# First slot's row list from match matrices, strided q and k loaded as runs of two tokens, idle matmuls at the head, low words on VectorE

## The chip, the core and the metric

One core of a Trainium2 chip runs one program. TensorE (PE in the profile) multiplies, VectorE (DVE) and ScalarE (ACT) do the elementwise work and empty PSUM, GpSimd (POOL) does some elementwise work and issues the indirect DMAs (gather, scatter), and SyncE (SP) issues most plain DMAs. Each engine takes its instructions in the order in which they were planned. The metric is the device time of one execution in microseconds; lower is better.

## The reference, cut to what matters

```python
B, H, S, HD = 4, 8, 576, 64
# heads 0-3: local mask, 32 wide; heads 4-7: strided mask, same position modulo 32
attn = softmax(where(mask, q @ k.T / 8, -1e9)) @ v
x = attn.transpose(0, 2, 1, 3).reshape(2304, 512)
logits = x @ w_gate                       # 512 x 8
e = argmax(logits); gate = softmax(logits)[e]; g2 = sigmoid((x @ w_output_gate)[e])
y[t] = gate[t] * g2[t] * relu(x[t] @ w1[e]) @ w2[e]          # per token, one expert of 8
h = relu(y @ w_in); out = (h * h) @ w_out                     # 512 -> 2048 -> 512
```

## The kernel before

**Attention.** Four batches b. Each loads q, k, v (`load`, L232), turns q and k on TensorE and empties PSUM by `evac` (`transposes`, L276), and then runs units: nine "l" units for the local heads in five steps, and four pieces a0, a1, b0, b1 for the strided heads. `unit` and `piece_s`/`unit_s` make scores and softmax, `unit2` turns the probabilities, `unit3` multiplies by v and writes the result, transposed, to `xT`. The order of the steps is written in `ORDER`; `evac` gives every second copy to ScalarE and every second to VectorE. In the strided heads one partition holds 18 neighbouring tokens, so the transposed tiles `qsT`, `ksT`, `qlT`, `klT` are written with a stride of nine words.

**Routing, in the same stage.** Whenever 128 tokens are complete, `gates` (L499) multiplies them by the identity and the gate weights (`rw`, L509), empties them to `xr`, adds up the logits (`lg`), and stores the rows to `x_d` in DRAM (SP, L529). Tokens go in four groups, `GROUPS = [(0,4),(4,9),(9,13),(13,18)]`. `route` (L661) picks the expert, and counts each token's place in its expert's list (`posi`, through the matmuls `rk`). `scatter` (L730, POOL) writes token numbers at these places into the table `tab_d` in DRAM.

**The first slot.** After tile 12, `largest` (L572) finds the expert that has most tokens so far. Its list of rows is read back from `tab_d` (`rows_of`, L543), its first 208 rows are gathered from `x_d` (`win_get`, L547), and turned to `xh`, `xl` (L614 to L618). The rest of the slot comes from the last five tiles without a list: `late_rows` (L631) multiplies their high and low words `xa`, `xb` by match matrices `pm` (L649), on top of the gathered rows' own part (L623). `early_load` (L558) issues the list, the first two weight chunks `r` and the gathers, and is called by the scatter of tile 12. Its tiles lie where the front part of the attention's memory was.

**The experts.** Eight slots, in falling order of their counts; three-pass fp32r matmuls (`mm3`, L970 to L972) with high words `hw` from ScalarE (L950) and low words `lw` from VectorE (L954). Then the last two layers by a two-level scheme of seven products.

**What sets the order around the change.** A planner places every instruction by its own estimate of time; `tc.issue_after` pins one behind another on its engine. In the code before, the first two `hw` follow the last attention unit's copy, and the `lw` follow the last `pm`. The low words `xb` of tiles 13 to 17 are GpSimd's (`LPOOL`).

Of the kernel before, what the change touches and what calls it, by code (L numbers as in the profile page):

```python
# [20 lines left out]
P = 128  # L21
# [37 lines left out]
LPOOL = (13, 14, 15, 16, 17)  # L59
# [3 lines left out]
LWP = 0  # L63

# [28 lines left out]
C_END = C_TRI + P  # L93
# [3 lines left out]
def make_consts():  # L97
# [13 lines left out]
    c[:, C_TRI : C_TRI + P] = p[:, None] < p[None, :]  # L111
    c[:, C_IDX : C_IDX + NTILE] = p[:, None] + P * np.arange(NTILE)[None, :]
# [12 lines left out]
def moe_kernel(ctx, tc, q, k, v, wg, wog, w1, w2, w_in64, w_out64, consts, out, dbg=None):  # L125
# [9 lines left out]
    msk = big.tile([P, C_END - C_ML], F32, name="msk")  # L135
# [3 lines left out]
    ident = cst[:, C_ID : C_ID + P]  # L139
    cstb = big.tile([P, C_END - C_BF], BF16, name="cstb")  # L140
# [3 lines left out]
    trib = cstb[:, C_TRI - C_BF :]  # L144
    onesb = big.tile([P, P], BF16, name="onesb")
    nc.vector.memset(onesb, 1.0)
# [22 lines left out]
    zrow = big.tile([1, D], F32, name="zrow")  # L169
# [54 lines left out]
    for i in range(NPT):  # L224
# [5 lines left out]
        nc.vector.memset(x, 0.0)  # L230
# [4 lines left out]
    def load(b):  # L235
# [4 lines left out]
        for nm, src in (("q", q), ("k", k)):  # L240
            t[nm + "s"] = x = fro.tile([P, NS * HD], F32, name=f"{nm}s{b}", tag=nm + "s", bufs=1)
# [32 lines left out]
    def transposes(b, t):  # L274
        t.update(trs[b % 2])
        for kind in "sl":  # L276
            for n0 in range(0, 9, 3):
                for nm in ("q", "k"):
# [3 lines left out]
                    for i in range(3):  # L282
# [5 lines left out]
                        nc.tensor.transpose(ps[:, i, :], src, ident)  # L288
# [9 lines left out]
                    evac(y.rearrange("d h (g n) -> d n h g", n=9)[:, n0 : n0 + 3], z, 0.125 if nm == "q" else None)  # L298
# [53 lines left out]
    def piece_s(b, t, u, a):  # L352
# [3 lines left out]
        if a == 0:  # L356
            scs[b, u] = pss.tile(G, F32, name=f"sc{nm}", tag="sc")
            nc.tensor.matmul(
                flat(scs[b, u]),
                identb,  # L360
# [1078 lines left out]
```

## Time and profile before

| | us |
|---|---|
| median of 3 runs | 808.07 (807.59 to 809.14) |
| the profiled execution, its own time | 810.12 |
| its span in the profile | 808.2 |
| TensorE busy | 755.3 (93%) |
| VectorE busy | 554.9 (69%) |
| ScalarE busy | 467.4 (58%) |
| GpSimd busy | 192.1 (24%) |
| mean granted TensorE clock | 0.984 |

The span is the time between the first and the last instruction that the profiler shows; 1.9 us lie around it. TensorE's busy time contains pipelined matmuls whose ends are modelled, so a busy TensorE may still be waiting a little. The granted clock is 1.00 at 2.4 GHz and 0.50 at 1.2 GHz.

### The profile page before, as it was taken

To read this page: it belongs to the slowest core of one execution; us is meant where nothing else is said; L and a number is where in the kernel's file an instruction comes from. 1 tells how busy PE (TensorE), PEld (TensorE's weight loads), DVE (VectorE), ACT (ScalarE), POOL (GpSimd) and SP (SyncE) were. 2 spreads that over 40 slices of the span, in tenths; PEclk is the share of its full clock that TensorE was granted. 3 is DMA by queue.
4 is the path that set the end of the run, shared out by engine and by line. 5 is a ranking of instruction groups with operands and counts; after the bars stand their busy time and mean duration, and the time that the engine had idled before them with its cause. 6 is when DMAs were issued, how large, how long until landed. Compare 5 with 4: busy or idle time off the path is not lost.

```text
span 808.2 us, 14396 instructions
## 1 busy us (share of the span) xinstructions
PE 755.3 (93%) x5355; PEld 679.8 (84%) x5355; DVE 554.9 (69%) x1034; ACT 467.4 (58%) x930; POOL 192.1 (24%) x183
## 2 busy tenths in 40 slices
PE   4789999499999999999989999999999999999994
PEld 3667777499999999999977888888898988899893
DVE  6758867554548578779898778787554688566542
ACT  3746746234546456656686667666655586556443
POOL 4102122635075654531132221004000003000002
PEclk9999999689999999999999999999999999999998
DMA  9995611729479998976545633524232225212002
GB/s 193 202 194 146 142 54 29 237 71 340 165 174 292 172 331 295 309 248 198 178 170 161 210 125 127 177 87 150 92 106 89 72 98 182 86 73 97 21 1 82
DMA packets 105410, 124.83 MB, mean 154 GB/s; under 512 B 42801, under 2 KB 77137, under 8 KB 105330
## 3 DMA queue, kind: packets, MB, share of 16 engines
q1 hardware_dynamic: 95746, 100.77, 42.9%
q0 software_dynamic: 8096, 22.63, 8.5%
q8 instruction: 44, 0.72, 0.4%
q10 hardware_dynamic: 1488, 0.42, 0.2%
q14 instruction: 36, 0.29, 0.2%
HBM read 101.67 MB, written 22.12 MB: 153 GB/s over the span
## 4 chain that ended last, share of the span: by engine, by line
PE 53%; issue 17%; DMA 10%; DVE 9%; ACT 5%; POOL 4%; SPq 1%; POOLq 0%; ACTq 0%; DVEq 0%
PE o L970 4%; PE o L972 4%; DMA s0wo<-in_moe_w_out_dram 4%; PE o L971 4%; PE h L970 3%; PE h L971 3%; PE h L972 3%; PE y L970 3%; PE y L971 3%; PE y L972 3%; PE rw L509 2%; DMA ws_d<-sa 1%; POOL idx_d L862 1%; DMA idx_d<-toki,cpi 1%; PE lr L649 1%
## 5 line engine op out<-in xcount | busy, mean ns | idle before, releaser
L970 PE MATMUL o<-hwo,gh 128*128 128x512 f32 x288 | 114.5, 398 | 5.1 <-ACT gh L1098 5.1
L971 PE MATMUL o<-lwo,gh 128*128 128x512 f32 x288 | 113.4, 394 | 0.0
L954 DVE TENSOR_TENSOR lw<-rw,hw 128x1024 fp32r<-128x1024 f32 x62 | 79.0, 1274 | 44.6 <-ACT hw L950 41.6
L1184 ACT ACTIVATE rl<-rl 128x384 f32<-128x384 f32 x96 | 49.5, 518 | 94.7 <-DVE rl L1182 94.6
L950 ACT ACTIVATE hw<-rw 128x1024 fp32r<-128x1024 f32 x62 | 65.8, 1062 | 65.5 <-PE h L971 44.8
L972 PE MATMUL o<-hwo,gl 128*128 128x512 f32 x288 | 85.1, 396 | 2.0 <-DVE gl L1099 2.0
L1099 DVE TENSOR_TENSOR gl<-rl,gh 128x384 fp32r<-128x384 f32 x96 | 58.0, 606 | 41.9 <-ACT gh L1098 40.8
L1215 POOL DMA_INDIRECT out_dram<-ob,idx x18 | 20.6, 1147 | 273.9 <-ACT ob L1214 269.2
L970 PE MATMUL h<-xh,hw 128*128 128x416 f32 (+7 forms) x256 | 81.0, 316 | 1.5 <-DVE hl L1070 1.3
L972 PE MATMUL h<-xh,lw 128*128 128x416 f32 (+7 forms) x256 | 79.4, 310 | 0.0
L971 PE MATMUL h<-xl,hw 128*128 128x416 f32 (+7 forms) x256 | 79.4, 310 | 0.0
L971 PE MATMUL y<-hl,hw 128*128 128x416 f32 (+7 forms) x256 | 77.1, 310 | 0.0
L972 PE MATMUL y<-hh,lw 128*128 128x416 f32 (+7 forms) x256 | 76.6, 310 | 0.0
L970 PEld LDWEIGHTS o<-hwo,gh 128*128 128x128 f32 x288 | 54.0, 188 | 17.6 <-ACT gh L1098 8.6
L970 PE MATMUL y<-hh,hw 128*128 128x416 f32 (+7 forms) x256 | 68.0, 311 | 0.2 <-ACT hh L1069 0.2
L972 PEld LDWEIGHTS o<-hwo,gl 128*128 128x128 f32 x288 | 53.6, 188 | 13.1 <-DVE gl L1099 3.4
L971 PEld LDWEIGHTS o<-lwo,gh 128*128 128x128 f32 x288 | 54.1, 188 | 9.0
L1098 ACT ACTIVATE gh<-rl 128x384 fp32r<-128x384 f32 x96 | 49.9, 521 | 1.8
L970 PEld LDWEIGHTS h<-xh,hw 128*128 128x128 f32 x256 | 48.1, 188 | 3.2 <-DVE hl L1070 2.9
L1185 ACT ACTIVATE rl<-rl 128x384 f32<-128x384 f32 x96 | 49.5, 519 | 1.7
L971 PEld LDWEIGHTS h<-xl,hw 128*128 128x128 f32 x256 | 48.2, 188 | 0.3 <-DVE xl L659 0.2
L971 PEld LDWEIGHTS y<-hl,hw 128*128 128x128 f32 x256 | 48.1, 188 | 0.1
(597 smaller groups left out, 1917.4 us busy)
## 6 DMA issues: line engine op xcount, KB each, us to landing
rw<-in_moe_w_dram SPq DMA_DIRECT2D x62, 512.0 KB
rwa<-ws_d SPq DMA_DIRECT2D x24, 512.0 KB
rwb<-ws_d SPq DMA_DIRECT2D x24, 384.0 KB
e6wi<-in_moe_w_in_dram SPq DMA_DIRECT2D x32, 256.0 KB
rwo<-wout_d SPq DMA_DIRECT2D x16, 512.0 KB
x_d<-xr SPq DMA_DIRECT2D x18, 256.0 KB
ws_d<-eo POOLq DMA_DIRECT2D x16, 256.0 KB, 4.9
s0wo<-in_moe_w_out_dram SPq DMA_DIRECT2D x8, 512.0 KB
```

The source lines that it names most:

```text
L509: nc.tensor.matmul(ps[:, kk, :], xT[:, kd, col : col + P], igw[:, kd, :], start=True, stop=True)
L649: nc.tensor.matmul(ps[:, a, :], parts[t][x][:, 2 * h + a, :], pm, start=False, stop=(t == NTILE - 1 and a == x == 1),)
L950: nc.scalar.activation(hi, raw, AF.Copy)
L954: eng.tensor_tensor(lo, raw, hi.bitcast(F32), op=ALU.subtract)
L970: kept(nc.tensor.matmul(ps, ah, bh, start=first, stop=False))
L971: kept(nc.tensor.matmul(ps, ah, bl_, start=False, stop=False))
L972: kept(nc.tensor.matmul(ps, al, bh, start=False, stop=last))
L1098: nc.scalar.activation(h, x, AF.Copy)
L1099: nc.vector.tensor_tensor(l, x, h.bitcast(F32), op=ALU.subtract)
L1184: nc.scalar.activation(rl[:, :HC], src, AF.Relu)
L1185: nc.scalar.activation(rl[:, :HC], rl[:, :HC], AF.Square)
L1215: ins = nc.gpsimd.indirect_dma_start(out=out[:, :], out_offset=bass.IndirectOffsetOnAxis(ap=idx[:, gt_, 0:1], axis=0), in_=ob, in_offset=None,
```

## The change

- **Row list.** `match_tiles` makes, for each tile below 13, a 128 x 128 matrix that marks the low seven bits of each token's place (`pmh`), and keeps the rest (`posm`). `match_rows` compares the rest with the list's columns, multiplies by token numbers, and adds 13 small matmuls into one PSUM tile, from which `ix0` is made. The first slot no longer reads `tab_d`. `early_load` moves out of the scatter to the main loop, and the scatters of the last two groups follow the gathers on GpSimd (`put_place`).
- **Strided q and k.** A partition holds nine runs of two tokens (512 bytes); each tensor is loaded by four DMAs, one a head, where there was one of 4608 bytes a partition. The transposed tiles are then written without a stride; `ksT` has its two halves apart. The local heads' q and k are laid out alike. Batch 0's strided k goes through ScalarE's queue.
- **Idle matmuls.** `turn_over` issues 10 matmuls of 512 columns ahead of everything, and two after each group of batch 0's strided transposes.
- **Low words.** `xb` is VectorE's for all of tiles 13 to 17; those of 16 and 17 follow the last `pm`.
- **Order.** The first two `hw` follow the last `xa`; the first slot's transposes follow the last `rw`; some memsets move to GpSimd; slot 1's transposes come one step later.

```diff
-LPOOL = (13, 14, 15, 16, 17)
+LPM = (16, 17)
+HEAD = (10, 2)
...
+    pairs = lambda src, b, h: src[b, 4 + h].rearrange("(n g u) d -> g n (u d)", g=32, u=2)
+    ks0 = fro.tile([P, S * 4 // P * HD], F32, name="ks0", tag="ks", bufs=1)
+    for h in (0, 2, 1, 3):
+        nc.scalar.dma_start(ks0[32 * h : 32 * h + 32].rearrange("p (n c) -> p n c", c=2 * HD), pairs(k, 0, h))
...
+    def turn_over(n, ins=None):
+        for _ in range(n):
+            with tc.issue_after(ins.ins) if ins else nullcontext():
+                ins = nc.tensor.matmul(
+                    idle, onesb, onesb[:, None, :].to_broadcast([P, 4, P]), start=True, stop=True
+                )
+
+    turn_over(HEAD[0])
...
-            go(x, src[b, 4:8].rearrange("h (g n) d -> (h g) (n d)", n=NS))
+            for h in (0, 2, 1, 3):
+                go(x[32 * h : 32 * h + 32].rearrange("p (n c) -> p n c", c=2 * HD), pairs(src, b, h))
...
-                go(x[h // 2 * HD : h // 2 * HD + HD, :, h % 2, :], src[b, h].rearrange("(g n) d -> g n d", n=NL_))
+                go(x[h // 2 * HD : h // 2 * HD + HD, :, h % 2, :], src[b, h].rearrange("(n g) d -> g n d", n=NL_))
...
-                        y = y.rearrange("d h (g n) u -> d n h g u", n=9)[:, n0 : n0 + 3]
+                        y = y.rearrange("d h u (n g) -> d u n h g", n=9)[:, :, n0 : n0 + 3]
                         for j in range(2):
                             r = slice(j * HD, (j + 1) * HD)
-                            evac(y[r, :, :, :, j], z[r])
+                            evac(y[r, j], z[r])
...
-                nc.scalar.activation(xa, xr[:, :, :P], AF.Copy)
-                eng = nc.gpsimd if t in LPOOL else nc.vector
-                eng.tensor_tensor(xb, xr[:, :, :P], xa.bitcast(F32), op=ALU.subtract)
+                lead["xa"] = nc.scalar.activation(xa, xr[:, :, :P], AF.Copy)
+                low = lambda xa=xa, xb=xb, xr=xr: nc.vector.tensor_tensor(
+                    xb, xr[:, :, :P], xa.bitcast(F32), op=ALU.subtract
+                )
...
+    def match_tiles(b, ts):
+        T = len(ts)
+        sl = slice(ts[0], ts[0] + T)
+        hi = wk.tile([P, 5], I32, name=f"hi{b}", tag="hi", bufs=1)
+        nc.vector.tensor_scalar(hi[:, :T], posi[:, sl], P - 1, None, op0=ALU.bitwise_and)
+        hf = wk.tile([P, 5], F32, name=f"hf{b}", tag="hf", bufs=1)
+        nc.vector.tensor_copy(hf[:, :T], hi[:, :T])
+        for i, t in enumerate(ts):
+            nc.vector.tensor_scalar(
+                pmh[:, t, :], cstb[:, C_IA - C_BF : C_TK - C_BF], hf[:, i : i + 1], None, op0=ALU.is_equal
+            )
+        nc.vector.tensor_tensor(posm[:, sl], posi[:, sl], hf[:, :T], op=ALU.subtract)
...
+    def match_rows():
+        rel = wk.tile([P, LATE], F32, name="relm", tag="relm", bufs=1)
+        nc.vector.tensor_scalar(rel, posm, lead["base"], None, op0=ALU.subtract)
...
+        for t in range(LATE):
+            nc.tensor.matmul(
+                ips.rearrange("p e r -> p (e r)"),
+                pmh[:, t, :],
+                wt[:, t].rearrange("p e r -> p (e r)"),
+                start=(t == 0),
+                stop=(t == LATE - 1),
+            )
...
     def early_load():
+        match_rows()
         e0 = lead["e0"]
         oreg[0] = nc.values_load(e0[0:1, :], engines=[ET.SP], min_val=0, max_val=E - 1)
-        lead["ix"] = rows_of(0, oreg[0])
...
-                for a in range(KD):
-                    nc.tensor.transpose(ps[:, a, :c], w[:c, a, :], ident[:c, :c])
+                with tc.issue_after(lead["rw"].ins):
+                    for a in range(KD):
+                        nc.tensor.transpose(ps[:, a, :c], w[:c, a, :], ident[:c, :c])
...
+        with tc.issue_after(lead["pm"].ins):
+            while lows:
+                lows.pop(0)()
...
-            if t == LATE - 1:
-                early_load()
...
-        with tc.issue_after(last_ev["s"].ins) if first else nullcontext():
+        with tc.issue_after(lead["xa"].ins) if first else nullcontext():
             nc.scalar.activation(hi, raw, AF.Copy)
...
-            if f == 4 and k + 1 < E:
+            if f == (5 if k == 0 else 4) and k + 1 < E:
                 win_split(k + 1)
```

## Rows read from the trace of the kernel before

**Rows 1.** Busy time by stretch: span, then PE, PEld, DVE, ACT, POOL, clock, DMA share, GB/s
```profile
0.00:26.20 26.20, 12.74 (x173) 8.93 (x173) 17.68 (x33) 8.30 (x11) 10.01 (x15) 1.00 1.00 209
...
42.00:142.90 100.90, 94.56 (x1418) 74.16 (x1418) 75.37 (x239) 58.53 (x192) 17.73 (x21) 1.00 0.49 110
142.90:169.00 26.10, 15.53 (x80) 14.63 (x81) 12.85 (x23) 6.05 (x11) 15.57 (x14) 0.61 0.57 184
169.00:808.00 639.00, 619.49 (x3490) 571.82 (x3488) 437.90 (x712) 381.44 (x668) 146.67 (x130) 1.00 0.50 157
```

**Rows 2.** Chain that ended last, 140 to 170 us: start, length, what
```profile
140.70 2.17 PE rw L509 x16
...
157.50 3.85 PE lr L623 x16
161.47 7.72 PE lr L649 x40
```

**Rows 3.** Timeline, the first slot's list: start, length, engine, line, operation, idle before it
```profile
130.58 0.18 DVE L697 TENSOR_REDUCE posi<-pp 128x4 int32<-128x32 f32 x1
132.64 0.15 DVE L595 TENSOR_REDUCE base<-tb 128x1 f32<-128x8 f32 x1
...
135.12 0.97 POOL L730 DMA_INDIRECT tab_d<-tok,posi  x1 [0.30 <-issue]
...
141.14 0.44 SPq L543 DMA_DIRECT2D ix<-tab_d  x1
...
145.30 0.99 POOL L547 DMA_INDIRECT win<-x_d,ix  x1 [9.21 <-issue]
...
151.34 1.12 PE L614 MATMUL wt<-cst,win 128*128 128x128 f32 x4 [8.49 <-DMA win<-x_d,ix]
```

**Rows 4.** Busy time of a 2 us stretch inside the gap
```profile
148.00:150.00 2.00, 0.00 (x0) 0.00 (x0) 0.26 (x1) 1.56 (x4) 1.69 (x2) 0.50 1.12 333
```

**Rows 5.** Timeline, the last group's route and the first slot's words
```profile
146.71 1.06 ACT L950 ACTIVATE hw<-r 128x1024 fp32r<-128x1024 f32 x1 [5.49 <-DMA r<-in_moe_w_dram]
...
150.01 6.17 POOL L519 TENSOR_TENSOR xb<-xr,xa 128x512 fp32r<-128x512 f32 x5
...
150.70 0.20 DVE L665 TENSOR_REDUCE mx<-lg 128x5 f32<-128x40 f32 x1
150.93 5.31 DVE L667 TENSOR_TENSOR d<-lg,mx 128x40 f32<-128x40 f32 x1
...
158.27 1.31 DVE L637 TENSOR_SCALAR pm<-cst,rel 128x208 fp32r<-128x208 f32 x5
...
159.50 1.08 DVE L618 TENSOR_TENSOR xl<-wt,xh 128x512 fp32r<-128x512 f32 x2
...
160.50 2.35 DVE L954 TENSOR_TENSOR lw<-r,hw 128x1024 fp32r<-128x1024 f32 x2
```

**Rows 6.** Timeline, small bf16 matmuls on one PSUM tile
```profile
129.83 0.22 PE L684 MATMUL rk<-oh,onesb 128*128 128x24 bf16 x3
```

**Rows 7.** Groups by shape, ScalarE: copies with and without a stride, mean ns
```profile
L272 ACT ACTIVATE ksT<-ts1k 64x384 f32<-64x384 f32 x3 | 2.7, 890 | 0.1
...
L272 ACT ACTIVATE pts2l<-pt2l 96x512 f32<-96x512 f32 x3 | 1.8, 592 | 0.5 <-PE pt2l L409 0.5
```

**Rows 8.** Timeline and waits at the head: three transposes each, and TensorE's waits
```profile
5.26 0.90 PE L288 MATMUL ts0q<-cst,qs 128*128 128x128 f32 x3 [5.26 <-DMA cst<-in_consts_dram]
...
26.28 0.52 PE L288 MATMUL ts1q<-cst,qs 128*128 128x128 f32 x3 [3.27 <-DMA qs<-in_q_dram]
```

**Rows 9.** Waits of TensorE, 26 to 143 us: waited in total, times, longest
```profile
PE tl1q L288 <- DMA vsp<-in_v_dram: 1.6, 1, 1.6
```

**Rows 10.** DMA queue: packets, MB, share of 16 engines; in 0.5:5, 9:15 and 108:121 us
```profile
q1 hardware_dynamic: 211, 0.90, 53.9%
...
q1 hardware_dynamic: 3349, 1.04, 121.8%
...
q1 hardware_dynamic: 1023, 0.51, 13.1%
```

More of the change, by code (lines that the diff above doesn't have):

```diff
@@ L92 @@
 C_TRI = C_MS + SM
[L93 removed]
+C_IA = C_TRI + P
+C_TK = C_IA + P
+C_END = C_TK + 2 * LATE
 C_BF = C_ML - P
@@ L287, in transposes @@
                             src = x[:, n].rearrange("p j d -> p (j d)")
-                        nc.tensor.transpose(ps[:, i, :], src, ident)
+                        ins = nc.tensor.transpose(ps[:, i, :], src, ident)
+                    if b == 0 and kind == "s":
+                        turn_over(HEAD[1], ins)
+                        lead["ts"] = ins
                     y = t[nm + kind + "T"]
@@ L357, in piece_s @@
             scs[b, u] = pss.tile(G, F32, name=f"sc{nm}", tag="sc")
-            nc.tensor.matmul(
-                flat(scs[b, u]),
-                identb,
-                cstb[:, None, C_MS - C_BF : C_MS - C_BF + SM].to_broadcast([P, n_s, SM]),
-                start=True,
-                stop=False,
-            )
+            with tc.issue_after(lead["ts"].ins) if b == 0 else nullcontext():
+                nc.tensor.matmul(
+                    flat(scs[b, u]),
+                    identb,
+                    cstb[:, None, C_MS - C_BF : C_MS - C_BF + SM].to_broadcast([P, n_s, SM]),
+                    start=True,
+                    stop=False,
+                )
         sc = scs[b, u]
@@ L473, in drain, with put_place @@
                 while scq:
-                    scq.pop(0)[1]()
+                    put_place()
+    def put_place():
+        _, fn, g = scq.pop(0)
+        with tc.issue_after((last_ev["p"] if g < 2 else lead["win"]).ins):
+            fn()
     carry = [None]
@@ new lines, in match_rows @@
+    def match_rows():
+        rel = wk.tile([P, LATE], F32, name="relm", tag="relm", bufs=1)
+        nc.vector.tensor_scalar(rel, posm, lead["base"], None, op0=ALU.subtract)
+        eq = wk.tile([P, LATE, NW], F32, name="eqm", tag="eqm", bufs=1)
+        nc.vector.tensor_tensor(
+            eq,
+            rel[:, :, None].to_broadcast([P, LATE, NW]),
+            cst[:, None, C_PJ : C_PJ + NW].to_broadcast([P, LATE, NW]),
+            op=ALU.is_equal,
+        )
+        wt = wk.tile([P, LATE, 2, NW], BF16, name="wtm", tag="wtm", bufs=1)
+        tk = cstb[:, C_TK - C_BF : C_END - C_BF].rearrange("p (t e) -> p t e", e=2)
+        nc.vector.tensor_tensor(
+            wt,
+            eq[:, :, None, :].to_broadcast([P, LATE, 2, NW]),
+            tk[:, :, :, None].to_broadcast([P, LATE, 2, NW]),
+            op=ALU.mult,
+        )
+        ips = pss.tile([P, 2, NW], F32, name="ips", tag="tp")
+        for t in range(LATE):
+            nc.tensor.matmul(
+                ips.rearrange("p e r -> p (e r)"),
[3 more added lines that the diff above has]
+                stop=(t == LATE - 1),
+            )
+        lead["ix"] = ix = const.tile([P, NW], I32, name="ix0")
+        i2 = wk.tile([P, NW], F32, name="i2", tag="i2", bufs=1)
+        nc.vector.tensor_copy(i2, ips[:, 1])
+        nc.vector.scalar_tensor_tensor(out=ix, in0=ips[:, 0], scalar=float(P), in1=i2, op0=ALU.mult, op1=ALU.add)
@@ L697, in route @@
             nc.vector.tensor_reduce(posi[:, ts[0] : ts[0] + T], pp[:, :T], axis=AX.X, op=ALU.add)
+        if ts[0] < LATE:
+            match_tiles(b, ts)
         cn = wk.tile([P, E], F32, name=f"cn{b}", tag="cn", bufs=2)
@@ L779, in moe_kernel @@
                 )
-            if scq and nun[0] >= scq[0][0] and (b < B - 1 or "ok" in lead):
-                with tc.issue_after(last_ev["p"].ins):
-                    scq.pop(0)[1]()
+            if b == B - 1 and n >= LN and early and "do" in lead:
+                lead.pop("do")()
+                early_load()
+                lead["ok"] = 1
+            if scq and nun[0] >= scq[0][0] and (scq[0][2] < 2 or "ok" in lead):
+                put_place()
             for _ in range(TN[b][n]):
```

50 lines of the change are left out of this document (31 added, 19 removed).

## The prediction

> **What bounds the kernel now.** I read the busy times by stretch first, to see which stretches TensorE doesn't fill [rows 1]. From 169 us to the end it works 619.5 of 639 us at the full clock: whatever starts that stretch earlier ends the kernel earlier by as much, since nothing in it hangs on a fixed time. From 42 to 142.9 it idles 6.3 of 100.9 us. Between them lie 26.1 us with 15.5 us of work and a mean granted clock of 0.61. Then the chain of waits for this gap [rows 2], and the timelines of what feeds it [rows 3, 5]. The reader is to see three things. The list makes a round trip: last scatter issued at 135.12, list read at 141.14, first gather at 145.30, first transpose of gathered rows at 151.34 [rows 3]. ScalarE waits 5.49 us for a weight chunk in front of the last copies of `xr`, so the last route begins only at 150.70; there one small VectorE instruction takes 5.31 us, its neighbour 0.20 us, while GpSimd makes the low words in 6.17 us [rows 5]. And TensorE, with nothing to do after 142.87, falls to the lower clock (0.50, which is 1.2 GHz), at which the 40 matmuls of L649 take 7.72 us [rows 2, 4].
>
> I call the end of the last `rw` T0 (142.87, 140.70 + 2.17 [rows 2]). The experts begin at about 169.2 (161.47 + 7.72), T0 + 26.3.
>
> **Part 1, the list.** The last places that it needs are known at 130.76, the fullest expert's base at 132.79 [rows 3]. New behind them on VectorE: seven instructions of `match_tiles` for tiles 9 to 12, of which most can lie before the base, then `rel`, `eq`, `wt`; then 13 matmuls, then two more. Small VectorE instructions take 0.15 to 0.20 us [rows 3, 5], three small bf16 matmuls 0.22 us [rows 6]: 0.7 + 1.0 + 0.4 = 2.1 us, so 134.9 at the soonest. VectorE is busy there and I allow 2 us for the queue: list at 137. The queue is what nothing in this trace bounds well: 0 to 5 us. GpSimd's four gathers need 1.3 us each (0.97 + 0.30 [rows 3]), so 137 to 142. From a gather's issue to its transposes went 151.34 - 145.30 = 6.0 us, beside a DMA load of 333 GB/s [rows 3, 4]; at that price the first rows are there at 143.0, the fourth at about 146.9. Transposes and L623 then run beside the route and not after it. Taken off the path: the scatters, the reading and the wait. The nine scatters of the last two groups now stand behind the gathers on GpSimd; who waits for them is the second slot's list on SP and the weight loads queued behind it. Five of them need the last places (about T0 + 3.6), so they end near T0 + 10 and land 6 us later (135.12 to 141.14 [rows 3]), some 6 us after the experts begin; the slot's transposes move one step back. I cost that at 0; if the cover fails, at 1 to 2 us. The new waits hold TensorE (the matmuls wait for `wt`, `rw` matmuls queue behind): 0.5 us, at most 2.
>
> **Part 2, ScalarE and the low words.** With the `hw` behind the last `xa`, the last `xr` copy and its sum end near T0 + 1.5. From 150.70 to the last `pm` (158.27 + 1.31) the route took 8.9 us, of which 5.1 is the 5.31 us instruction beyond a normal 0.20 [rows 5]: 3.8 us remain, last `pm` at T0 + 5.3. Moved to VectorE: two low words behind the `pm`. One is 512 words wide; 1024 cost 1.18 us (2.35 / 2), so 0.6 us each. Behind the `pm` now stand 1.2 (low words), 1.08 (`xl`), 2.35 (`lw`) and one 0.5 for the first half of `lr`: 5.1 us, T0 + 10.4. TensorE beside it: L623 at the full clock half of 3.85 for its last 16, L649 half of 7.72, 3.9 us, so T0 + 5.3 + 0.7 + 3.9 = T0 + 9.9 at the soonest. VectorE is therefore late next, by a little. Experts at T0 + 10.4, bounds 9.0 (some `lw` placed ahead of the `pm`) and 13 (waits between these). **Gain 26.3 - 10.4 = 15.9 us**, bounds 13.3 and 17.3. The other three low words cost 1.8 us of VectorE before T0, where it waits for TensorE anyway; if not, up to 1.8 us.
>
> **Part 3, the loads.** At the head DMA is full (share 1.00 to 26.2 us [rows 1]), and TensorE waits twice for it, 3.27 us for batch 1's q and 1.6 us for its local q [rows 8, 9]. Before, a strided tensor is 128 packets of 4608 bytes: 0.539 x 4.5 us x 16 engines / 211 packets = 184 ns each [rows 10], 1.47 us a tensor. After, 1152 of 512 bytes. The nearest row is the stores of `xr`, whose packets have that size: 0.131 x 13 x 16 / 1023 = 26.6 ns, 1.92 us a tensor, 0.45 more. In the crowd, packets of mostly 256 bytes take 1.218 x 6 x 16 / 3349 = 34.9 ns: 2.51 us, 1.04 more. Between them I take 0.7. Four tensors (batches 0 and 1) lie before the two waits: **2.8 us lost**, bounds 1.8 and 4.2. The other four load where the DMA share is 0.49 [rows 1]: 0; without that cover another 2.8. ScalarE's queue for batch 0's k gains nothing, the DMA engines being what is full.
>
> The page "DMA: Bandwidth & Descriptors" of the Trainium skill, section Specifications, sets the size from which a transfer runs at line rate at 512 bytes. By that rule the runs of two tokens cost nothing; the trace has 512 bytes in 26.6 ns and 4.3 KB in 184 ns [rows 10], so the larger packet is 1.2 times as fast a byte, but the small ones are stores.
>
> **Part 4, the copies.** Copies with a stride take 890 ns for 384 words, 592 for 512 without one [rows 7]: about 0.47 without, 0.4 saved. There are 15 a batch, 60 in all, half on ScalarE: 12 us an engine over the attention. New on VectorE: 22 instructions of `match_tiles`, 4 us. But the path is TensorE's, which idles only 6.3 us from 42 on [rows 1]; I take **2.0 us gained**, bounds 0 and 5. Part 1's 0.5 us of new waits goes against it.
>
> **Part 5, the rest, at 0.** The idle matmuls: 512 columns by L649's rate (7.72 / 40 for 208 columns, at half clock) are 0.47 us, 0.24 at full clock; 10 + 12 of them lie where TensorE waits for data (first transposes at 5.26 [rows 8]). They bring the transposes from 0.90 to the 0.52 us per three of later [rows 8], but the next DMA wait takes that back. Without the cover 12 x 0.24 = 2.9 us. The memsets go to GpSimd, busy 10 of the first 26.2 us [rows 1].
>
> **The sum**, against the profiled execution's own 810.12 us (span 808.2): - 15.9 + 2.8 - 2.0 + 0.5 = - 14.6, so 795.5. The median is 2.05 lower, 808.07: **793.5 us**. Adding the bounds of the large terms: gain between 10 and 20 us, 788 to 798.
>
> **Rivals.**
> 1. *The list comes late.* If it is ready at 140 and not 137, the fourth gather ends at 145, its rows are used at 151, TensorE has too little in between, and the clock falls as it does now [rows 4]. Then L623 ends near 153 and L649 takes its 7.72 us: experts at 161.2, T0 + 18.3, 7.9 us later than forecast: 801.4. For it: VectorE's full queue at 130 to 134. Against: 2 us of allowance are in the sum. 0.17.
> 2. *Small packets are dearer.* At 50 ns, 3.6 us a tensor, 2.1 more than before, 8.5 us for four instead of 2.8: 799.2. Against: both nearest rows lie below 35 ns. 0.08.
> 3. *Small packets are free.* With 0 for 2.8: 790.7. For it: the rows that price them are stores and 256-byte reads, no read of 512. 0.12. This is what the Trainium skill's rule above would give.
> 4. *The copies were the path.* Their whole 5 us and more: 789.5. For it: VectorE and ScalarE are busy 75 and 59 us of 42 to 142.9, and busy TensorE rows may hide short waits [rows 1]. Against: TensorE's own 94.56 us there. 0.08.
> 5. *Slower.* One mechanism, the strided loads: if all eight tensors lie on the path, attention becomes a DMA stage. Without part 3 the gain is 17.4 us; it turns into a loss of 0.2% from 2.4 us a tensor, which is 54 ns a packet. At 60 ns: 2.85 x 8 = 22.8, so 813.5. Against: the 0.49 share, twice the dearest row. 0.05.
> 6. *It doesn't do what it says:* the experts begin early, but wait for their next weights or the second list, and give it back: 808. Against: these loads are issued relative to the same events. 0.03.
>
> **How the numbers follow.** My forecast has 0.47. Its own spread and rivals 1 to 4 lie between 787.5 and 802; outside are 5, 6 and the tails, some 0.15. A measurement of this kernel tells about 0.2% from no change. Faster by more: 0.47 + 0.17 + 0.08 + 0.12 + 0.08 = 0.92; within: 0.03; slower: 0.05.
>
> **What would show it.** Right: first gather at 136 to 138, no SP read of `tab_d` before it; the last route's second instruction at 0.2 us; clock 1.00 throughout 140 to 170; L649 some 0.11 us apart; experts near T0 + 10, T0 between 141 and 147. Part 3: batch 1's first transposes 1 to 3 us later than 26.28. Part 4: the copies at 0.45 to 0.55 us. Wrong: any stretch of clock 0.50 after T0, or a T0 beyond 148.

## The result and the profile after

| | before | after |
|---|---|---|
| median, us | 807.83 (805.80 to 809.14, 4 runs) | 797.32 (796.06 to 798.41, 4 runs) |
| the profiled execution, its own time | 810.12 | 796.06 |
| its span | 808.2 | 794.3 |
| mean granted clock | 0.984 | 0.985 |

The ratio is 0.9872, 95% interval 0.9846 to 0.9897: faster by 1.3%, 10.5 us. The forecast was 793.5, range 787.5 to 802.

The busy times by stretch come first, cut at the same events as in [rows 1] (span, then PE, PEld, DVE, ACT, POOL, granted clock, DMA share, GB/s):

```profile
0.00:26.20 26.20, 19.48 (x224) 11.79 (x224) 12.75 (x25) 6.78 (x18) 13.14 (x19) 0.87 1.07 175
...
42.00:140.70 98.70, 94.98 (x1432) 74.24 (x1431) 74.87 (x267) 53.74 (x195) 16.55 (x20) 1.00 0.62 135
140.70:157.40 16.70, 13.28 (x83) 12.43 (x81) 10.88 (x30) 5.16 (x10) 12.36 (x10) 0.69 0.80 203
157.40:794.30 636.90, 618.44 (x3490) 571.85 (x3488) 436.69 (x712) 381.95 (x668) 148.63 (x130) 0.99 0.49 158
```

The gap between the last `rw` (T0) and the experts shrank from 26.1 us to 16.5, and its clock is still 0.69 and not 1.00. T0 itself is at 140.87 for 142.87, and the stretch behind is 2.3 us shorter. So 13.9 us of span: 2.0 ahead of T0, 9.6 in the gap, 2.3 behind it. The timeline of the gap (start, length, engine, line, operation, idle time before it):

```profile
136.03 0.48 PE L637 MATMUL ips<-wtm,pmh 128*128 128x8 bf16 x13
136.37 4.50 PE L547 MATMUL rw<-igw,xT 128*128 128x144 f32 x32
140.70 0.60 PE L705 MATMUL wt<-cst,win 128*128 128x128 f32 x4
142.43 0.50 PE L705 MATMUL wt<-cst,win 80*128 80x80 f32 x4 [1.12 <-DMA win<-x_d,ix]
...
145.77 2.08 PE L714 MATMUL lr<-cst,win 128*128 128x128 f32 x8 [1.00 <-DMA win<-x_d,ix]
148.60 1.91 PE L714 MATMUL lr<-cst,win 32*128 32x32 f32 x8 [0.75 <-DMA win<-x_d,ix]
...
138.65 4.38 SPq L574 DMA_DIRECT2D x_d<-xr  x5
143.28 2.38 SPq L1037 DMA_DIRECT2D rw<-in_moe_w_dram  x3
```

And the chain of waits through it (start, length, what), with the last gather's landing and the matmuls on the late rows:

```profile
137.18 0.99 POOL win L592
...
141.00 7.55 DMA win<-x_d,ix
...
150.63 6.92 PE lr L743 x40
```

The round trip of [rows 3] is gone: the list comes out of 13 matmuls of 0.48 us together, and the first gather starts at 137.18 for 145.30. VectorE's long route instruction of [rows 5] is gone too (0.20 for 5.31 us), and the low words follow:

```profile
143.14 0.20 DVE L759 TENSOR_REDUCE mx<-lg 128x5 f32<-128x40 f32 x1
143.37 0.20 DVE L761 TENSOR_TENSOR d<-lg,mx 128x40 f32<-128x40 f32 x1
...
145.54 1.45 DVE L728 TENSOR_SCALAR pm<-cst,rel 128x208 fp32r<-128x208 f32 x5
...
149.10 2.35 DVE L1047 TENSOR_TENSOR lw<-r,hw 128x1024 fp32r<-128x1024 f32 x2
```

What is left of the gap is mostly the rows: TensorE waits 1.12, 1.00 and 0.75 us for the second, third and fourth gather (and 0.54 us for the route), and in these waits the clock falls, as it did in [rows 4]. In steps of 2 us:

```profile
140.00:142.00 2.00, 1.30 (x12) 1.06 (x10) 2.00 (x6) 2.00 (x6) 1.57 (x2) 1.00 0.89 204
142.00:144.00 2.00, 1.36 (x12) 1.24 (x12) 1.86 (x8) 2.00 (x4) 1.51 (x2) 1.00 1.09 326
144.00:146.00 2.00, 0.67 (x8) 0.54 (x9) 1.76 (x10) 1.34 (x3) 1.70 (x2) 0.79 1.04 314
146.00:148.00 2.00, 1.85 (x8) 1.55 (x8) 2.00 (x6) 0.00 (x0) 1.39 (x3) 0.50 1.24 300
```

TensorE works 1.30, 1.36 and 0.67 of 2 us after T0, then it is at 0.50, the 1.2 GHz level, until about 155. The 40 matmuls of L743 (L649 before) fall into that and take 6.92 us.

### The profile page after: what moved, and what is told of

The parts are those of the page before. It is cut to its first block, busy times and chain, and to the rows that moved or that the text cites. A ratio compares the mean times of both kernels' runs of the same rounds, so it can differ in the third digit from the quotient of the medians.

```text
span 794.3 us, 14515 instructions
## 1 busy us (share of the span) xinstructions
PE 759.1 (96%) x5390; PEld 680.2 (86%) x5390; DVE 545.3 (69%) x1061; ACT 458.0 (58%) x930; POOL 192.8 (24%) x182
## 4 chain that ended last, share of the span: by engine, by line
PE 63%; issue 18%; DMA 5%; DVE 5%; ACT 4%; POOL 3%; SPq 0%; POOLq 0%; ACTq 0%; DVEq 0%
PE o L1063 5%; PE o L1065 5%; PE o L1064 5%; PE h L1063 4%; PE y L1064 4%; PE h L1064 4%; PE y L1063 4%; PE h L1065 4%; PE y L1065 4%; DMA s0wo<-in_moe_w_out_dram 3%; PE rw L547 2%; DMA qs<-in_q_dram 1%; POOL idx_d L955 1%; DMA win<-x_d,ix 1%; POOL out_dram L1308 1%
## 5 line engine op out<-in xcount | busy, mean ns | idle before, releaser
L1047 DVE TENSOR_TENSOR lw<-rw,hw 128x1024 fp32r<-128x1024 f32 x62 | 77.4, 1248 | 45.8 <-ACT hw L1043 42.8
L1065 PEld LDWEIGHTS h<-xh,lw 128*128 128x128 f32 x256 | 48.2, 188 | 0.1
```

The lines of the kernel that those rows point to most:

```text
L1047: eng.tensor_tensor(lo, raw, hi.bitcast(F32), op=ALU.subtract)
L1065: kept(nc.tensor.matmul(ps, al, bh, start=False, stop=last))
```

## The experiments

Every run stands against the kernel before, run beside it on the same chip; ratios are to be compared, not microseconds. "Behind T0" is the time from the last `rw` to the first expert matmul, "rest" from there to the end of the span; both come from the one profiled execution. (In a_oldlayout 16 matmuls of `rw` stand behind the first `lr`, so its T0 isn't comparable.)

| run | ratio (95%) | T0 | behind T0 | rest |
|---|---|---|---|---|
| before | 1 | 142.9 | 26.1 | 639.2 |
| after | 0.9872 (0.9846 to 0.9897) | 140.9 | 16.5 | 636.9 |
| a_warm | 0.9874 (0.9848 to 0.9900) | 144.6 | 13.3 | 643.7 |
| a_stearly | 0.9883 (0.9857 to 0.9909) | 144.5 | 17.8 | 638.6 |
| a_gfirst | 0.9976 (0.9952 to 1.0000) | 152.6 | 15.8 | 641.7 |
| b_lowhw | 0.9993 (0.9975 to 1.0010) | 155.6 | 20.1 | 637.6 |
| a_bigload | 0.9839 (0.9811 to 0.9867) | 137.4 | 15.9 | 638.5 |
| a_oldlayout | 0.9921 (0.9892 to 0.9950) | 154.2 | 12.4 | 640.0 |
| a_nohead | 1.0006 (0.9986 to 1.0025) | 150.6 | 16.2 | 641.6 |
| a_h10_0 | 0.9982 (0.9961 to 1.0003) | 149.8 | 17.2 | 639.1 |
| a_h0_2 | 0.9940 (0.9909 to 0.9970) | 144.1 | 15.4 | 643.0 |
| a_h20_2 | 0.9891 (0.9861 to 0.9921) | 145.0 | 15.0 | 637.1 |
| a_blwarm | 0.9840 (0.9795 to 0.9886) | 140.7 | 13.0 | 641.6 |
| a_best | 0.9850 (0.9830 to 0.9869) | 144.9 | 19.5 | 642.0 |

The kernel before took 808.9 and 809.5 us in the first two batches and 816.4 in the third (a_gfirst, b_lowhw, a_oldlayout, a_best), on another chip. There the traces of the changed kernels show waits that nothing in them explains, such as these in the strided scores (the cause is named "issue") and a longer issue of the five stores (4.38 us in the changed kernel). Two rows of a_best:

```profile
111.48 0.39 PE L405 MATMUL sc3s<-ksT,qsT 128*18 128x36 f32 x9 [1.09 <-issue]
...
142.66 7.54 SPq L574 DMA_DIRECT2D x_d<-xr  x5
```

So absolute places of that batch say nothing about the others.

### The gap: clock, stores, gathers, route

**a_warm.** Idle matmuls of 512 columns hold the clock while the rows land: `stay_up` puts n of them behind the transposes of the first 128 rows and behind each step of `lr<-win`.

```diff
+WARM = (4, 4, 4, 4)
...
+    def stay_up(n, ins):
...
+                if t == 0:
+                    stay_up(WARM[0], ins)
...
+                stay_up(WARM[t], ins)
```

> The changed kernel with 16 more idle matmuls of 512 bf16 columns, four behind each step of the gathered rows' work (first transposes, and L714 of the second, third and fourth gather). Theory: after T0 TensorE is only half busy, the granted clock falls to 0.50 at about 145 and stays there until 155, and the 40 matmuls of L743 take 6.9 us; with the gaps filled the clock stays at 1.00, the 40 take about 4.5 us, and the experts begin 2.5 to 4 us sooner: 793 to 795 us. Rival 1: the waits for gathers are the whole loss and the clock only their result; the idle matmuls delay the real ones (16 x 0.24 = 3.8 us at most): 796 to 800 us. Rival 2: the clock falls all the same: 797 to 801 us.

The clock stays at 1.00 from T0 to beyond the experts' start. Its 2 us steps, then the first matmul on the late rows and the first one of the experts:

```profile
144.00:146.00 2.00, 0.88 (x8) 0.67 (x7) 2.00 (x7) 1.18 (x3) 1.39 (x3) 1.00 0.86 253
146.00:148.00 2.00, 2.00 (x18) 1.42 (x16) 1.79 (x8) 1.62 (x4) 1.69 (x2) 1.00 1.06 327
...
153.32 0.34 PE L756 MATMUL lr<-pm,xa 128*128 128x208 f32 x1
...
157.86 0.37 PE L1076 MATMUL h<-xh,hw 128*128 128x416 f32 x1
```

The 40 matmuls take 4.5 us for 6.9, the experts begin 13.3 us behind T0 for 16.5. That the clock is what made them slow is shown. But the time is the changed kernel's, where the theory had 793 to 795 us. The 3.2 us saved in the gap are 0.4%, and the two ratios, each within ±0.26%, leave open about 0.37% (3.0 us) between them; so that the saving went elsewhere is likely, not shown. The profiled execution shows where it can go: it lost 3.7 us ahead of T0 and 6.8 behind the experts' start. Ahead of T0 the clock falls behind the wait for batch 1's q, where the changed kernel's stays up. Behind the experts' start it has a wait of 2.55 us at 179.43 and another of 1.23 at 408.69, and each time the clock falls behind it. The changed kernel's trace has no fall in this stretch, though it has the second wait too (1.21 us at 401.60):

```profile
32.00:34.00 2.00, 2.00 (x16) 1.48 (x16) 0.53 (x2) 1.90 (x10) 0.38 (x1) 0.50 0.98 199
...
178.00:180.00 2.00, 0.57 (x3) 0.56 (x4) 1.38 (x2) 0.14 (x2) 2.00 (x1) 1.00 1.06 373
180.00:182.00 2.00, 2.00 (x9) 1.94 (x8) 1.03 (x1) 1.34 (x2) 2.00 (x1) 0.62 1.04 318
...
179.43 0.46 PE L1076 MATMUL h<-xh,hw 128*128 128x416 f32 x1 [2.55 <-DVE hl L1176]
```

Whether these losses come with the idle matmuls or with the execution can't be told from one profile a kernel; a_stearly falls behind batch 1's q and loses at 408 in the same way without them.

**a_stearly.** The five late stores leave the gap: the rows of tiles 13 to 17 are not stored at all, and tiles 8 to 12 store theirs a second time in their place, ahead of the gathers.

```diff
-            stq(x_d[1 + t * P : 1 + (t + 1) * P, :], xr[:, :, :P])
+            if t < LATE:
+                stq(x_d[1 + t * P : 1 + (t + 1) * P, :], xr[:, :, :P])
+            if NTILE - 5 - 5 <= t < LATE:
+                stq(x_d[1 + (t + 5) * P : 1 + (t + 6) * P, :], xr[:, :, :P])
```

> The changed kernel, but the five stores of the last tiles' rows (1.25 MB, issued at 138.65 to 143.0 us, beside the gathers) are taken out of that stretch: tiles 8 to 12 store their rows twice instead, the second time at the rows of tiles 13 to 17, so these rows of the table hold other tokens' words. Theory A, the gathers are late because stores and weight loads share the 16 DMA engines with them: the fourth gather lands some 5 us after its issue and not 7.6, TensorE's waits after T0 (140.65) shrink from about 4 us to under 2, the experts begin 2 to 4 us sooner, 793 to 795 us. Theory B, the gathers are slow by themselves (GpSimd makes their descriptors): landings as before, 796 to 798 us.

No gain: 17.8 us behind T0, and a ratio of 0.9883 for 0.9872. With the stores away the three weight loads moved up, to 139.34, ahead of the first gather (140.80), and its rows were used only at 148.47, 7.7 us after issue. Something else took the place of the traffic that was removed.

**a_gfirst.** As a_stearly, and the weight loads wait until the fourth gather has landed (a one-column copy from its buffer into theirs). The experts' next weights thus come later than in the changed kernel, so the whole time is no measure here; the gap is.

```diff
+            if ngp[0] < 3:
+                ngp[0] += 1
+                with tc.issue_after(lead["xa"].ins):
+                    nc.scalar.activation(raw[:32, 0, :1], wins[0, 3][:32, 0, :1], AF.Copy)
             nc.sync.dma_start(raw, src)
```

> The changed kernel, with nothing that loads or stores beside the gathers but the first two weight chunks: the five late stores are moved ahead (tiles 8 to 12 store twice, so some rows of x_d hold other tokens), and the next three weight loads wait until the fourth gather's rows have landed. In the changed kernel the gathers took 3.3 to 7.6 us from issue to use, beside five stores and three weight loads at a DMA share of about 1.0; without the stores alone the weight loads moved up, and the first took 7.7 us. Theory 'crowd': what slows the gathers is this traffic; alone they land 3 to 3.5 us after their issue, the matmuls on the late rows begin some 7.5 us behind the last rw for 9.8, the experts 12 to 13.5 us behind it for 16.5. Theory 'own': an indirect gather takes 4.5 us and more by itself, experts at 15.5 to 17 behind the last rw. The whole time is no verdict here, since the next weight chunks come some 10 us later than the experts want them: 795 to 808.

Gathers, first uses, and VectorE's next route instruction:

```profile
150.21 0.96 POOL L596 DMA_INDIRECT win<-x_d,ix  x1 [0.30 <-issue]
...
152.89 0.66 PE L709 MATMUL wt<-cst,win 128*128 128x128 f32 x4 [0.29 <-issue]
153.95 0.50 PE L709 MATMUL wt<-cst,win 80*128 80x80 f32 x4 [0.40 <-DMA win<-x_d,ix]
...
160.42 0.20 DVE L793 TENSOR_TENSOR pp<-rk,oh 128x40 f32<-128x40 f32 x1 [3.96 <-PE lr L718]
```

Without the stores and the later weight loads (the first two chunks still ran), the second gather landed 3.7 us after issue (150.21 to 153.95), and TensorE waited for rows only once, 0.40 us. So much of "crowd" holds. Yet the experts start 15.8 us behind T0, not 12 to 13.5: TensorE waited 0.74 and 1.05 us for the route instead, VectorE's `pp` came 3.96 us late, and the clock fell at about 156 all the same. The profile names L718 as what `pp` waited for; in the changed kernel `pp` followed the `rk` at once. Why it didn't here stays open; the run belongs to the batch with the unexplained waits. Clearing the traffic alone doesn't clear the gap.

**b_lowhw.** The kernel before with part 2 alone (but the low words of tiles 16 and 17 don't wait for the last `pm`).

```diff
-LPOOL = (13, 14, 15, 16, 17)
+LPOOL = ()
...
-        with tc.issue_after(last_ev["s"].ins) if first else nullcontext():
+        with tc.issue_after(lead["xa"].ins) if first else nullcontext():
```

> The kernel before with part 2 alone: the low words of tiles 13 to 17 on VectorE, the first two hw behind the last xa; list, loads, copies and head as before. Theory 'two conditions': the route is done near 147, but the list still makes its round trip, the gathers still start at 145.3 and the clock still falls, so the two stretches of the gap end on the gathers: fourth rows at about 155, L623 3.85 us and L649 7.72 us at the lower clock behind, experts near 167 for 169: 805 to 807.5 where before is 808. Rival 'route alone': the route carried most of the gap by itself, 799 to 802.

Nothing that can be measured, so the rival "route alone" (799 to 802) is out. VectorE's long instruction is gone here too (`d` at 156.92 takes 0.20 us), and yet the route stood still, since the last two `xa` stand behind the copy of the gathered rows on ScalarE in this plan:

```profile
153.23 0.99 POOL L547 DMA_INDIRECT win<-x_d,ix  x1 [10.22 <-PE o3l L433]
...
160.08 0.66 PE L614 MATMUL wt<-cst,win 128*128 128x128 f32 x4 [4.47 <-DMA win<-x_d,ix]
...
160.77 0.60 ACT L616 ACTIVATE xh<-wt 128x512 fp32r<-128x512 f32 x1 [5.20 <-PE wt L614]
161.26 0.62 ACT L517 ACTIVATE xa<-xr 128x512 fp32r<-128x512 f32 x1
```

Without the early list the gathers end the gap whatever the route does. So part 2 by itself brings nothing here. Part 1 by itself was not run, and how the 9.6 us that the gap lost split between the parts stays open.

### Loads and copies

**a_bigload.** The strided heads' loads and layout as before (4608-byte rows, copies with a stride), the local heads' new layout kept.

```diff
-            for h in (0, 2, 1, 3):
-                go(x[32 * h : 32 * h + 32].rearrange("p (n c) -> p n c", c=2 * HD), pairs(src, b, h))
+            go(x, src[b, 4:8].rearrange("h (g n) d -> (h g) (n d)", n=NS))
```

> The changed kernel with the strided heads' q and k loaded as in the kernel before (one DMA a tensor, 4608 bytes a partition) and their turned tiles written with a stride of nine again; the local heads keep the new layout. Forecast's theory: four tensors cost 0.7 us each on the path, the strided copies give back 9 of 15 parts of 2.0 us: 1.6 us faster than the changed kernel, 795.5 us, batch 1's first transposes at 26 to 28 and not 30.7. Rival: the head's delay (4.4 us at batch 1's first transposes, gone by the local q at 42) costs nothing at the end, and only the copies count: 1 to 2 us slower, 798 to 800 us.

Batch 1's first strided transposes start at 27.8 us there, in the changed kernel at 30.7 behind a wait for q. The row of the changed kernel, then its DMA queue's packets, MB and share of 16 engines from 0.5 to 5 us, as [rows 10]:

```profile
PE ts1q L317 <- DMA qs<-in_q_dram: 2.9, 1, 2.9
...
q1 hardware_dynamic: 883, 0.43, 37.4%
```

A 512-byte packet took 0.374 x 4.5 x 16 / 883 = 30.5 ns, a tensor of 1152 of them 2.20 us for 1.47: 0.73 more, where I took 0.7. The ratios differ by 0.33% (2.7 us). This run's forecast was 1.6: 2.8 for the loads, less 1.2 for 9 of the 15 copies a batch, which get their stride back. The two intervals overlap, and 3% of TensorE's and VectorE's instructions stand elsewhere in this plan (counted here and below as those outside the longest order that the two traces share), so the price of part 3 on the whole time is likely, not shown. This kernel is the fastest of all that ran, with a_blwarm.

**a_oldlayout.** All q and k loaded and laid out as before; list, route and idle matmuls stay.

```diff
-            for h in (0, 2, 1, 3):
-                go(x[32 * h : 32 * h + 32].rearrange("p (n c) -> p n c", c=2 * HD), pairs(src, b, h))
+            go(x, src[b, 4:8].rearrange("h (g n) d -> (h g) (n d)", n=NS))
...
-                go(x[h // 2 * HD : h // 2 * HD + HD, :, h % 2, :], src[b, h].rearrange("(n g) d -> g n d", n=NL_))
+                go(x[h // 2 * HD : h // 2 * HD + HD, :, h % 2, :], src[b, h].rearrange("(g n) d -> g n d", n=NL_))
```

> The changed kernel with q and k of all heads loaded, laid out and copied as before (part 3 and part 4 undone; list, route, idle matmuls stay). Against the kernel with the strided heads' loads as before but the local heads' layout changed (0.984 of before), this prices the stride in the local heads' copies alone, and against the changed kernel (0.987) both parts. My prediction's terms: part 3 costs 2.8, part 4 brings 2.0, so 0.986, 796 to 797. Rival 'copies off the path': 0.983 to 0.984, part 4 brings nothing. Rival 'copies on the path': 0.988 to 0.991.

Against a_bigload 0.82% slower (intervals apart), though the two ran in different batches. In the same batch a_best is 0.71% faster, but it has more idle matmuls too. One group of ScalarE's copies in the changed kernel and one in this (busy, mean ns of one):

```profile
L301 ACT ACTIVATE ksT<-ts1k 64x384 f32<-64x384 f32 x3 | 1.5, 485 | 0.9 <-PE ts1k L317 0.9
```
```profile
L299 ACT ACTIVATE ksT<-ts1k 64x384 f32<-64x384 f32 x3 | 2.6, 873 | 0.7 <-DVE ksT L295 0.6
```

So the copies are longer again by 0.4 us each. That they are what the 0.82% pays for is not shown. The order of the plan changes with them: 7% of TensorE's and 13% of VectorE's other instructions stand elsewhere than in a_bigload, and the next section shows what a smaller change of order can cost. And in this run's gap TensorE waits 3.20 us ahead of the last 16 `rw` and 1.64 us among the 40 matmuls on the late rows with the cause "issue". The attention itself doesn't settle it. From batch 1's first strided to batch 3's first local transposes went 81.0 us in the kernel before (26.3 to 107.3) and 75.8 in the changed one (30.7 to 106.5), 77.9 here and 76.0 in a_best. But a_bigload, with 9 of 15 copies strided, takes 74.8, and a_nohead and a_h10_0 below, with none strided, take 81.0 and 81.4.

### The idle matmuls at the head

**a_nohead.** No idle matmuls.

```diff
-HEAD = (10, 2)
+HEAD = (0, 0)
```

> The changed kernel without the idle matmuls at the head (10 and 2 behind each of six groups of transposes). Theory: they run while TensorE waits for data; batch 0's transposes take 0.90 us instead of 0.52 to 0.87 for three, batch 1's wait for DMA hides it: 797 us, within 1 us. Rival 1: they hold the clock up where work is on the path: 2 us slower without them. Rival 2: the 12 between the transposes, at 0.53 us each in the low clock, delay the scores of batch 0: 1 to 3 us faster without them.

809.6 us: without them the whole gain is gone. The gap isn't where it went: that is 16.2 us here, but T0 lies at 150.6 for 140.9, and the rest takes 641.6 for 636.9. And with the idle matmuls goes the order of the plan. Of the other instructions 6% on TensorE and 9% on VectorE stand elsewhere in this kernel, because the planner counts the idle matmuls' time. Three more runs are to separate the two.

**a_h10_0**, `HEAD = (10, 0)`: the order of a_nohead, with the ten at the head.

> The changed kernel with the ten idle matmuls at the head, without the two behind each group of transposes. The other instructions then stand in the very order of the kernel without any idle matmuls (809.6 us). Theory 'clock': 797 to 801, since the head is kept busy as in the changed kernel. Theory 'order': 807 to 811.

**a_h0_2**, `HEAD = (0, 2)`: nearly the changed kernel's order, without the ten.

> The changed kernel without the ten idle matmuls ahead of everything; the two behind each group of batch 0's strided transposes stay. The order of the other instructions is then almost the changed kernel's (99% of TensorE's, VectorE's and ScalarE's instructions stand alike), while without any idle matmuls some 3 to 9% stand elsewhere. Two theories on why the changed kernel takes 809.6 us without idle matmuls and 797.3 with them. Theory 'clock': the idle matmuls hold the granted clock, and the ten carry most of it: 805 to 810 here, with the clock at 0.50 in more stretches of the attention than the changed kernel has. Theory 'order': what counts is where the planner puts the other instructions: 795 to 800 here.

**a_h20_2**, `HEAD = (20, 2)`: the changed kernel's very order, with 20.

> The changed kernel with 20 idle matmuls at the head for 10; every other instruction stands in the same order. In the changed kernel's trace the ten end at 5.4 us, the first strided q lands at 8.0, and the clock is 0.50 to 0.66 from 8 to 15. With 20 at 0.44 us each they end at 9.8. Theory 'clock': no 0.50 before 15 us, batch 0 done 2 to 3 us sooner, but the wait for batch 1's q (first transposes at 30.7) takes it back, as in the two kernels whose head ran at 1.00 and whose clock then fell at 30: 797 to 800. Theory 'order': 797 to 799, as the changed kernel. If the ends of these waits for q don't move, neither theory has the head's clock on the path.

a_h10_0 came out at 807.75, where "order" had it: the ten matmuls are back and the gain is not. Against a_nohead that is 0.24%, within the intervals. In this order TensorE loses, among others, twice (this kernel's waits from 26 to 150 us; the changed kernel has 2.9 and 0.5 there):

```profile
PE ts1q L317 <- DMA qs<-in_q_dram: 5.0, 1, 5.0
PE pt3l L442 <- DVE rc3l L369: 1.7, 1, 1.7
```

and its T0 is 9 us later. All of that is lost after the last idle matmul: batch 1 starts at 30.9, and at 31.1 in a_nohead, for 30.7 in the changed kernel. a_h0_2 (803.8) lies between the two theories; its runs spread from 799 to 811. a_h20_2 tells most. Its clock is 1.00 throughout the head, where the changed kernel's is at 0.66 and 0.50 (first row the changed kernel, second a_h20_2):

```profile
10.00:12.00 2.00, 1.38 (x5) 1.02 (x6) 0.00 (x0) 1.11 (x2) 2.00 (x4) 0.50 1.25 168
```
```profile
10.00:12.00 2.00, 1.57 (x10) 1.03 (x10) 0.00 (x0) 1.39 (x3) 2.00 (x4) 1.00 1.25 189
```

And it makes no difference: batch 1 starts at 30.4 for 30.7, batch 3's local heads at 106.2 for 106.5. The wait for q takes back what the head's clock gives. The head's idle matmuls bring nothing that can be measured by their clock; what the changed kernel owes them is, for the most part, an order of the plan. (No run has the changed kernel's order without the twelve between the transposes, so what these do themselves is argued from batch 1's start alone.)

What does differ between these two is one fall of the clock at 131 us. First a_h20_2, then the changed kernel, the same instruction and the stretch behind it:

```profile
130.62 0.61 PE L442 MATMUL pt3l<-cst,pr3l 128*96 128x128 f32 x4 [1.19 <-DVE pr3l L370]
...
132.00:134.00 2.00, 2.00 (x36) 1.96 (x36) 1.60 (x15) 0.69 (x1) 0.00 (x0) 0.50 0.03 8
```
```profile
130.18 0.61 PE L442 MATMUL pt3l<-cst,pr3l 128*96 128x128 f32 x4 [0.46 <-DVE pr3l L370]
...
132.00:134.00 2.00, 1.73 (x39) 1.49 (x35) 1.93 (x13) 1.06 (x2) 0.00 (x0) 1.00 0.03 8
```

A wait of 1.19 us for 0.46, and TensorE is at half clock until about 141: T0 at 145.0 for 140.9.

### Two combinations

**a_blwarm** is a_bigload with a_warm's 16 idle matmuls (both diffs above).

> The kernel with the strided heads' loads and layout as before (795.7 us, experts 15.9 us behind the last rw), and 16 idle matmuls between the last rw and the experts, four behind each step on the gathered rows, which in the changed kernel held the clock at 1.00 there (experts 13.4 us behind the last rw for 16.7). Theory: the two edits add up, 795.7 - 2.5 = 793.2, from 792 to 795. Rival: the idle matmuls lie on the path themselves (4 us of them) and give back what the clock brings, 795 to 797.

Experts 13.0 us behind T0 for 15.9, as expected, but the whole time didn't follow: the ratio is a_bigload's within 0.0001, where 2.5 us less were forecast (its interval is ±0.45%, 3.7 us). Its head ran at 0.50 from 8 to 18 us, its batch 1 began at 31.0 for 27.8.

**a_best** is the same with `HEAD = (20, 2)` and `WARM = (4, 3, 3, 0)`.

> The strided heads' loads and layout as before, 20 idle matmuls at the head for 10, and ten idle matmuls behind the first three steps on the gathered rows (4, 3, 3 for the 4, 4, 4, 4 of the run that gave 0.984 of before). In that run the head was at 0.50 from 8 to 18 us, which put batch 1 at 31.0 for 27.8. Theory: with the head at 1.00 and fewer idle matmuls on the path it comes to 0.977 to 0.981 of before, 791 to 794. Rival: where the clock falls changes from run to run, and 0.982 to 0.985 is all there is.

The head ran at 1.00, batch 1 began at 28.0, and the ratio stayed at 0.985. In its gap TensorE waited 2.68 us for the route, where ScalarE had stood 4.06 us ahead of the last copy of `xr` with the cause "issue", and the clock fell behind that. The rival was right. No version beats the changed kernel by more than the intervals leave open; a_bigload, a_blwarm and a_best all lie 0.2 to 0.3% lower.

## Why the prediction was right, and where it was not

The time fell within the range, 3.8 us above the forecast. Profile against profile the sum was 0.6 off (795.5 forecast, 796.06 measured); the rest is that the execution profiled of before lay 2.05 above its median and that of after 1.26 below. But the sum is close by luck, because its errors cancel: the gap gave 6.3 less than forecast (9.6 for 15.9), T0 came 3.3 sooner (142.87 + 1.3 forecast), and the stretch behind gave 2.3 that nothing had foreseen. The 3.3 belong to this execution: in a_stearly, a_warm and a_h20_2, whose instructions stand in the same order as far as T0, it lies at 144.5, 144.6 and 145.0, each time after a fall of the clock that the changed kernel's trace doesn't have. And the prediction's own sign of being wrong, a stretch of clock 0.50 after T0, is there.

| step | forecast | measured |
|---|---|---|
| first gather | 136 to 138 | 137.18 |
| T0 | 142.87 + 1.3 = 144.2 | 140.87 |
| lead of the first gather on T0 | 7.2 (not said, but implied) | 3.7 |
| issue to use of the four gathers | 6.0 each | 3.5 or less, 3.95, 6.0, 7.6 |
| last `pm` done | T0 + 5.3 | T0 + 6.1 |
| VectorE done with `lw` | T0 + 10.4 | T0 + 10.6 |
| late-row matmuls start | T0 + 6.0 | T0 + 9.6 |
| their 40 take | 3.9 | 6.9 |
| experts | T0 + 10.4 | T0 + 16.5 |
| a 512-byte tensor, more | 0.7 us | 0.73 us |
| copies without a stride | 470 ns | 484 to 558 ns |
| gain of the copies | 2.0 | not to be separated |
| the stretch behind | 0 | - 2.3 |

**Part 1: the list was right, its place against T0 was not.** This is the step that failed. The list came at the predicted microsecond, but I moved T0 by + 1.3 and left the list where it was. In the trace the two are tied: TensorE makes the list's 13 matmuls behind the attention's last products and then has 4.50 us of `rw` left. In the changed kernel, in a_warm, a_stearly, a_bigload, a_best and a_gfirst the first gather starts 3.7 us ahead of T0, wherever T0 lies (4.5 in a_h20_2, whose `rw` run partly at half clock; 3.2 in the other order of a_nohead and a_h10_0). So the fourth gather's rows come at T0 + 7.7 and not at T0 + 2.7, and the transposes and `lr` that should have run beside the route had waits between them. The fourth, of only 32 rows, also took 7.6 us, not 6.0, beside the stores and weight loads.

**The clock.** Rival 1 asked for a list at 140; the list was at 137, and the rival's picture came true all the same: too little work on TensorE after T0, clock at 0.50, the 40 matmuls at 6.9 us. That is 3.6 us by the later start and 3.0 by the clock, less the 0.5 that VectorE was to add: the 6.1 by which the experts miss T0 + 10.4. I had tied the fall to the hour of the list and not to the waits behind T0, of whatever kind. In a_h20_2 TensorE waits only 0.26 us for the gathers, then 1.42 for the route, and the clock is at 0.50 from 148 on:

```profile
148.50 0.21 PE L776 MATMUL rk<-oh,cstb 128*128 128x40 bf16 x1 [1.42 <-DVE oh L773]
```

The Trainium skill, page "TensorE: Matmul & The Clock Gate", section "HAM oscillation — how this bites in real kernels", tells of a kernel that falls back to the lower clock again and again because each short stretch of matmuls is followed by a wait for data. This case's trace agrees for the one fall in the gap, with 1.30, 1.36 and 0.67 of 2 us, waits of about 1 us for the gathers, and then 0.50.

**Part 2 was right to 0.2 us** on VectorE. But it was called late next "by a little", and TensorE was later by 5.9.

**Part 3 was right** in the price of a tensor. The wait came 4.4 us later than before (26.28 to 30.7), beyond the 1 to 3 I named; against a_bigload it is 2.9. And the 4.4 didn't reach T0: by batch 1's local heads they are gone (41.4 for 42.0). Rivals 2, 3 and 5 are out: 30.5 ns is neither 50 (rival 2) nor 20.4, at which nine packets would take the 184 of a large one (rival 3), and from 26 to 140 us TensorE waits for q or k only once, 2.9 us, so eight tensors didn't lie on the path. The rule of 512 bytes that the prediction took from the Trainium skill, page "DMA: Bandwidth & Descriptors", section Specifications, doesn't hold here at the level of packets: 30.5 ns for 512 bytes, nine of them 275, against 184 for the large ones.

**Part 4 stays open.** The copies did get shorter, 484 to 558 ns for some 850 to 890, but no run separates their worth from the order of the plan. The attention gained 5.2 us between batch 1's strided and batch 3's local transposes, near rival 4 (5 us and more, chance 0.08); with the same short copies a_nohead gained none of it, and a_bigload, with most of them long, gained 6.2. So neither the 2.0 nor rival 4 is shown. The argument against that rival, TensorE's own 94.56 us of 100.9, was weak: the page counts matmuls as busy that wait, which I had said myself.

**Part 5.** Idle matmuls at 0: right for their clock (a_h20_2), wrong in what it left out. The ten cost 0.44 us each and not 0.24, the twelve 0.53 at half clock and 0.3 at full, and by the planner they moved up to 9% of the other instructions. Without the two behind each group the kernel is 1.1% slower (a_h10_0), without any 1.3% (a_nohead). The prediction took the order as given.

**Open.** Why the stretch behind the experts' start is 2.3 us shorter: in all profiles it lies between 636.9 and 643.7. Whether, and why, the 3 us that a held clock saves in the gap show in no total. What part 4 brings. And what in the order of a_nohead costs its 9 us at T0: its clock falls at 30 to 38, 112 to 117 and 140 to 143 us, and 2 us times the missing share, summed over the 2 us steps, is 6.8 us, at most what these falls cost; the rest isn't traced.

## What to carry to other kernels

When a change moves two events, ask what ties them: an instruction's place in its engine's queue, not its microsecond, says how far ahead of another it will be. Price short work that is spread between waits at the lower clock, and count the fall as a case of its own. In a planned kernel, an instruction that does nothing still moves others: compare the orders before you say what it is worth.

## What the runs showed of the hardware

- Whether the clock falls behind a short wait changes from execution to execution. Behind the wait for batch 1's q the changed kernel stays at 1.00, while a_stearly, whose TensorE instructions stand in the very same order, runs at 0.50 for the next 6 us. The changed kernel, then a_stearly:

```profile
30.00:32.00 2.00, 1.32 (x14) 1.09 (x16) 0.33 (x1) 0.76 (x4) 0.00 (x0) 1.00 1.08 201
```
```profile
30.82 0.87 PE L317 MATMUL ts1q<-cst,qs 128*128 128x128 f32 x3 [2.95 <-DMA qs<-in_q_dram]
...
32.00:34.00 2.00, 2.00 (x20) 1.48 (x18) 0.53 (x2) 1.91 (x10) 0.74 (x1) 0.50 0.98 162
```

- A single wait of 1.2 us, with TensorE partly busy around it, went ahead of a fall three times (a_h20_2 at 131, a_warm and a_stearly at 408), and once not (the changed kernel at 401). Falls lasted 3 to 14 us, 20 in the gap of the kernel before, and executions of one kernel spread by 2 to 12 us.
- A gather of rows of 2 KB took 3.5 to 7.7 us from issue to use (128 rows in 7.7, 32 rows in 7.6), the shorter times where fewer loads and stores lay beside it.
- Ten idle matmuls of 512 columns took 0.44 us each at a granted clock shown as 1.00, in the first 5 us of the kernel; those in a_warm's gap took 0.26 (1.03 for four), and two of them at 0.50 took 1.06. So the 1.00 shown for the first microseconds is doubtful: the times are nearer to the lower level. The same holds for the kernel before, whose transposes at 5.26 took 0.90 us [rows 8], as three do at 0.50. In the changed kernel:

```profile
1.05 4.38 PE L218 MATMUL idle<-onesb 128*128 128x512 bf16 x10 [1.05 <-DVE onesb L152]
...
14.27 1.06 PE L218 MATMUL idle<-onesb 128*128 128x512 bf16 x2
```
